# Twenty-one 8 KB buffers with 1 MB transfers, and 2 MB more of second-layer weights loaded early

## The chip, the cores and the metric

The kernel runs on one core of a Trainium2 chip. The metric is the device time of one execution in microseconds (us). Everything is fp32. The other cores of the chip have no part in it.

## The reference

Two things are computed one after the other. First a two-way attention between 512 tokens and 32 states, for 8 batches of 8 heads of width 64; then a soft mixture of experts over the 8 x (512 + 32) rows that come out, with 32 slots in 8 experts of 4.

```python
scores = scale * x @ state.T                # and the same scores the other way round
xread = softmax(scores, over states) @ state
sread = softmax(scores.T, over tokens) @ x
rows = concat([xread, sread])               # 4608 rows of 512
logits = rows @ phi                         # 512 x 32
slot_input = softmax(logits, over all rows).T @ rows
slot_out[e] = relu(slot_input[e] @ w1[e]) @ w2[e]     # w1: 8 x 512 x 1024, w2: 8 x 1024 x 512
out = softmax(logits, over slots) @ slot_out
```

The inputs are x (8.4 MB), the two weight tensors (16.8 MB each), the states and phi (0.6 MB); the output has 8.9 MB. Only x, the weights and the output matter for what follows.

## The kernel before

The program has four stages. The attention stage works through the 8 batches in an order that is written out by hand (the string `ORDER`, one step name per token); each engine executes its instructions in that order. A batch's step `R.b.1` is the last that reads the batch's x. The steps `Px`, `Ps` and `Y` towards the end of the stage gather the slot inputs, `windows` clears the two tiles `si_m` that hold them, and `SIe` fills these. The second stage multiplies them by the first-layer weights: `w1_part(hf, e)` for two halves `hf` of the hidden width and eight experts `e`, four matmul blocks each, 16 parts in all (matmuls at L650). The third stage multiplies by the second-layer weights: `w2_part(k, hf, e)` for four groups `k` of 128 output columns (matmuls at L710). The fourth, `out(k, q)` and `out_st(k)`, is interleaved with the third: it multiplies the combine weights by the slot outputs (L740), copies the result from PSUM by ScalarE (L749) and VectorE (L750), and stores it (L751).

All loads and nearly all stores are issued by SyncE (SP) in program order, and SP waits where a transfer's place or its source isn't ready. Two of the four transfers of the first batch's x are issued by ScalarE. The on-chip places for x, weights and outputs come from one pool, `big`: 43 buffers of 4 KB per partition (128 partitions, so 512 KB each), used in turn. One of them holds the states (`stT_sb`), 16 hold x (two per batch), and the remaining 26 take the first weights. Each weight tile is one transfer of 512 KB with rows of 4 KB per partition; 32 of them are w1, 32 are w2. After that a load waits for a place that comes free: `load_w(2)` follows each batch's `R.b.1`, one `load_w(1)` follows the last step that reads the states (`S.7` and `U.1`; the index `last` in the code), and `load_w(2)` follows each `w1_part`. So 43 weight tiles are on their way before the first `w1_part` frees a place: all 32 of w1, 11 of w2. The outputs take places of the same pool, two tiles and two stores of 512 KB for each `out(k, q)`.

Besides `big` there are the pool `wk` with 11 work tiles of 2 KB per partition under the tag `h` (the function `half`), and two tiles of 2 KB with the tags `srN` and `st`: turned read sums and turned states, last read by the steps `Ps.1` (L581) and `Px.3` (L501).

Of the kernel before, what the change touches and what calls it, by code (L numbers as in the profile page):

```python
# [8 lines left out]
F32 = mybir.dt.float32  # L9
# [6 lines left out]
P = 128  # L16
B = 8
S = 512
NS = 32
D = 64  # L20
E = 8
F = 1024
NJ = S // P
EPS = 1e-9
NBIG = 43
NH = 11


# [36 lines left out]
def attention_soft_moe(ctx: ExitStack, tc: tile.TileContext, x, stT, phi, w1, w2, out_x, out_s):  # L65
# [6 lines left out]
    nc = tc.nc  # L72
    pe, act, dve, pool = nc.tensor, nc.scalar, nc.vector, nc.gpsimd

    cp = ctx.enter_context(tc.tile_pool(name="const", bufs=1))
    ctx.enter_context(tc.manual_schedule())
    big = ctx.enter_context(tc.tile_pool(name="big", bufs=NBIG))


    stT_sb = big.tile([P, 4, 2, 2, 2, NS], F32, tag="big", name="stT_sb")  # L80
    phi_sb = cp.tile([P, 4, NS], F32, name="phi_sb")
    xb = []
    for b in range(B):
        for k in range(2):
            t = big.tile([P, 2, NJ, 2 * D], F32, tag="big", name=f"x{b}_{k}")
            xv = x[b].rearrange("p (g j c) -> p g j c", g=4, j=NJ)
            if b == 0:
                for g, eng in enumerate((nc.sync, act)):
                    eng.dma_start(t[:, g], xv[:, 2 * k + g])
            else:  # L90
                nc.sync.dma_start(t, xv[:, 2 * k : 2 * k + 2])
            xb.append(t)
        if b == 0:
            nc.sync.dma_start(stT_sb[:, 0:1], stT[:, 0:1])
        if b == 1:
            nc.sync.dma_start(stT_sb[:, 1:4], stT[:, 1:4])
            nc.sync.dma_start(phi_sb, phi)


    w1t, w2t = {}, {}  # L100
    todo = [(1, hf, e, k) for hf in range(2) for e in range(E) for k in range(2)]
    todo += [(2, k, e, 0) for k in range(4) for e in range(E)]

    def load_w2(t, k, e, ft):
        n = t.shape[1] // P
        t = t.rearrange("p (k f) -> p k f", k=n)
        nc.sync.dma_start(t, w2[e, k, :, ft : ft + n, :])
        for i in range(n):
            w2t[k, e, ft + i] = t[:, i]

    def load_w(n):
        for _ in range(min(n, len(todo))):
            layer, hf, e, k = todo.pop(0)
            t = big.tile([P, F], F32, tag="big", name=f"w{layer}_{hf}_{e}_{k}")
            if layer == 1:
                t = t.rearrange("p (k f) -> p k f", k=2)
                nc.sync.dma_start(t, w1[hf, e, :, 2 * k : 2 * k + 2, :])
                for i in range(2):
                    w1t[hf, e, 2 * k + i] = t[:, i]
            else:  # L120
                load_w2(t, hf, e, k)

    def st_t(b, g):
        return stT_sb[:, b // 2, g % 2, g // 2, b % 2, :]
# [2 lines left out]
    ident = cp.tile([P, P], F32, name="ident")  # L127
# [28 lines left out]
    with ExitStack() as actx:  # L156
        wk = actx.enter_context(tc.tile_pool(name="work", bufs=1))
# [14 lines left out]
        def half(name):  # L172
            return wk.tile([P, S], F32, tag="h", name=name, bufs=NH)

        def mtile(shape, name):
            return ps_m.tile(shape, F32, tag="ms", name=name)
# [24 lines left out]
        def X(b, g):  # L201
            r = R[b]
            r[f"xp{g}"] = p = ps_t.tile([P, S], F32, tag="tr", name=f"xt_ps{b}_{g}")
            for j in range(NJ):
                pe.transpose(p[:, P * j : P * j + P], xb[2 * b + g // 2][:, g % 2, j, :], ident)  # L205

        def xe(b, g):
            r = R[b]
# [100 lines left out]
        def R_(b, h):  # L309
            r = R[b]  # L310
            if h == 0:
                r["srp"] = mtile([P, 2, D], f"sr_ps{b}")
            for j in range(NJ):
                for g in range(4):
                    pe.matmul(  # L315
                        r["srp"][32 * g : 32 * g + 32, h, :],
                        r[f"eT{h}"][:, j, 32 * g : 32 * g + 32],
                        xb[2 * b + g // 2][:, g % 2, j, D * h : D * h + D],
                        start=(j == 0),
                        stop=(j == NJ - 1),  # L320
                    )
            if h == 1:
                load_w(2)

        def sr(b):
            r = R[b]
# [295 lines left out]
        def warm(n):  # L622
            p = ps_t.tile([P, S], F32, tag="tr", name=f"warm{n}_ps")
            pe.matmul(p[:, 0:n], ident, ident4[:, 0 : n // P], start=True, stop=True)

        steps = dict(
            G=G, Ge=Ge, X=X, xe=xe, S=Sc, q=q, m1=m1, sub=sub, x1=x1, l1=l1, r1=r1, mul=mul, aT=aT, m2=m2, e2=e2,
            l2=l2, E=E_, ee=ee, A=A_, ae=ae, R=R_, sr=sr, srT=srT, srTe=srTe, Lx=Lx, keep=keep, mx=mx, mk=mk,
            pv=pv, bm=bm, nme=nme, al=al, dx=dx, Lu=Lu, dT=dT, dTe=dTe, T=T_, tt=tt, U=U, Ue=Ue, Px=Px, Y=Y,
            Ls=Ls, Lse=Lse, Lr=Lr, msx=msx, als=als, dsx=dsx, Lus=Lus, lkp=lkp, D=Dn, V=V, Ve=Ve, Ps=Ps, Ys=Ys,  # L630
            Wd=Wd, We=We, Yf=Yf, SI=SI, SIe=SIe, windows=windows, mkd=mkd, ad=ad, W=warm,
        )
        load_w(NBIG - 2 * B - 1)
        order = ORDER.split()

        last = max(order.index(f"S.{B - 1}"), order.index("U.1"))
        for i, step in enumerate(order):
            name, *args = step.split(".")
            steps[name](*map(int, args))
            if i == last:  # L640
                load_w(1)


        h_ps = [ps_s.tile([P, 512], F32, tag="sc", name=f"h_ps{i}") for i in range(2)]
# [3 lines left out]
        def w1_part(hf, e):  # L648
            for kt in range(4):
                pe.matmul(  # L650
                    h_ps[hf][32 * kt : 32 * kt + 32, :],
                    si_m[kt // 2][:, 256 * (kt % 2) + 32 * e : 256 * (kt % 2) + 32 * e + 32],
                    w1t[hf, e, kt],
                    start=(e == 0),
                    stop=(e == E - 1),
                )
            load_w(2)

        def h_copy(hf):
            h_sb[hf] = half(f"h_sb{hf}")  # L660
# [19 lines left out]
        c = [half(f"c{i}") for i in range(3)]  # L680
        c = [v[:, 0 : t.shape[1]].rearrange("p (t n) -> p t n", n=NS) for v, t in zip(c, c_t)]
# [24 lines left out]
        def w2_part(k, hf, e):  # L706
            if hf == 0 and e == 0:
                so[k] = ps_s.tile([P, P], F32, tag="sc", name=f"so_ps{k}")
            for i in range(4):
                pe.matmul(  # L710
                    so[k][32 * i : 32 * i + 32, :],
                    h_m[hf][:, 256 * i + 32 * e : 256 * i + 32 * e + 32],
                    w2t[k, e, 4 * hf + i],
                    start=(hf == 0 and e == 0),
                    stop=(hf == 1 and e == E - 1),
                )
            if hf:
                load_w(1)

        def so_copy(k):  # L720
# [13 lines left out]
        def out(k, q):  # L734
            hf, col = k // 2, 128 * (k % 2)
            o = [(ps_t if j % 2 else ps_m).tile([P, 512], F32, tag="tr" if j % 2 else "ms", name=f"o{k}_{q}_{j}")
                 for j in range(NJ)]
            for j in range(NJ):
                rows = slice(32 * j, 32 * j + 32)
                pe.matmul(  # L740
                    o[j],
                    so_r[hf][rows, col : col + 128],
                    lt_all[rows, 4 * q : 4 * q + 4, :].rearrange("p b s -> p (b s)"),
                    start=True,
                    stop=True,
                )
            for jp in range(2):
                ot = big.tile([P, 2, 512], F32, tag="big", name=f"out{k}_{q}_{jp}")
                act.copy(ot[:, 0, :], o[2 * jp])  # L749
                dve.tensor_copy(ot[:, 1, :], o[2 * jp + 1])  # L750
                nc.sync.dma_start(out_x[k, q, jp].rearrange("p (i s) -> p i s", i=2), ot)  # L751

        ot = []

# [20 lines left out]
        for hf in range(2):  # L775
            for e in range(E):
                w1_part(hf, e)
                if hf == 0 and e == 5:
                    for i in range(3):
                        c_exp(i)  # L780
                if hf == 1 and e == 1:
                    h_turn(0)
                    h_relu(0)
                    for i in range(3):
                        c_div(i)
                if hf == 1 and e == 6:
                    for i in range(3):
                        c_back(i)
            h_copy(hf)

        for k in range(2):
            for e in range(E):
                w2_part(k, 0, e)
                if k == 0 and e == 3:
                    h_turn(1)
                    h_relu(1)
        for e in range(E):
            w2_part(0, 1, e)
        so_copy(0)

        for k in range(1, 4):
# [12 lines left out]
            more(2 * E)  # L814
            so_copy(k)
        out(2, 1)
        so_sum(3)
        out_st(2)
# [29 lines left out]
```

## Time and profile before

| | us |
|---|---|
| median of 3 runs | 135.07 (134.54 to 135.18) |
| profiled execution, whole time | 135.0 |
| profiled execution, span of the instructions | 133.2 |
| outside the span | 1.8 |

| engine | busy us | share of the span |
|---|---|---|
| TensorE matmuls (PE) | 118.0 | 89% |
| VectorE (DVE) | 86.8 | 65% |
| ScalarE (ACT) | 78.6 | 59% |
| GpSimd (POOL) | 44.7 | 34% |

The 16 DMA engines moved 51.76 MB, 389 GB/s over the span; TensorE's granted clock was at its full level throughout the work (mean 0.972 of it, since it falls after the last matmul). Matmuls are pipelined, so a busy PE need not be PE at its peak. The page cuts the span into 40 equal slices of 3.33 us; the views of the trace can be asked for any stretch, counted in us from the span's start.

### The profile page before, as it was taken

Reading aid. Unit: us, or ns where it says so; the run is one execution under the profiler, and the core shown is the slowest. Engines: PE = TensorE matmul, PEld = TensorE weight load, DVE = VectorE, ACT = ScalarE, POOL = GpSimd, SP = SyncE. Lnnn points to the kernel's source line nnn. Section 1 sums busy time; section 2 is a strip of 40 time slices with the busy share of each in tenths; the row PEclk is TensorE's granted clock in tenths of the full one; section 3 lists DMA queues with packets and bytes.
Section 4 is the critical chain, followed back from the end, with each engine's and each line's share of the span. In section 5 each row is a group of like instructions: output and inputs, shape, how many; then the busy total and the mean of one; then the engine's idle time right before and its main releaser. Section 6 shows DMA issues by size and latency. Waiting matters only on the chain.

```text
span 133.2 us, 5068 instructions
## 1 busy us (share of the span) xinstructions
PE 118.0 (89%) x2112; PEld 83.6 (63%) x2112; DVE 86.8 (65%) x218; ACT 78.6 (59%) x193; POOL 44.7 (34%) x64
## 2 busy tenths in 40 slices
PE   5898999999999999999899999999997999999200
PEld 2647686787886867567677779833893575754000
DVE  2019899999999999999997575059700733416300
ACT  3149999999999989988957414100100834427300
POOL 3006273563938056088884109406100000000000
PEclk9999999999999999999999999999999999999855
DMA  3999999999999999999999986999999999999992
GB/s 85 312 408 418 421 413 419 414 413 413 416 418 413 422 412 421 417 418 413 419 411 426 406 360 235 316 422 414 416 424 416 407 426 413 411 414 418 414 414 92
DMA packets 14854, 51.76 MB, mean 389 GB/s; under 512 B 1648, under 2 KB 1904, under 8 KB 14832
## 3 DMA queue, kind: packets, MB, share of 16 engines
q1 hardware_dynamic: 14544, 50.93, 95.2%
q10 hardware_dynamic: 288, 0.52, 1.1%
q8 instruction: 16, 0.26, 0.7%
q14 instruction: 6, 0.05, 0.1%
HBM read 42.53 MB, written 8.91 MB: 386 GB/s over the span
## 4 chain that ended last, share of the span: by engine, by line
PE 40%; DVE 37%; DMA 8%; issue 4%; ACT 2%; POOL 2%; DVEq 1%; ACTq 0%; POOLq 0%
PE so_ps L710 11%; PE h_ps L650 11%; PE o L740 7%; DVE l1s L248 6%; DVE q L232 6%; DVE nm L268 6%; DVE m L237 5%; DVE aT L262 5%; DMA phi_sb<-phi_in 5%; DMA x<-x_in 3%; DVE r L253 2%; POOL q L241 2%; PE os L758 2%; PE t_ps L467 1%; PE an_ps L287 1%
## 5 line engine op out<-in xcount | busy, mean ns | idle before, releaser
L750 DVE COPY out<-o 128x512 f32<-128x512 f32 x16 | 10.3, 686 | 18.7 <-PE o L740 18.7
L241 POOL TENSOR_TENSOR q<-q,m 128x512 f32<-128x512 f32 x16 | 16.7, 1050 | 16.0 <-DVE m L237 6.2
L210 ACT ACTIVATE xt<-xt_ps 128x512 f32<-128x512 f32 x32 | 18.9, 617 | 4.9 <-PE xt_ps L205 4.8
L257 POOL TENSOR_TENSOR q<-q,r 128x512 f32<-128x512 f32 x16 | 16.7, 1048 | 8.2 <-ACT eT L295 2.3
L205 PE MATMUL xt_ps<-ident,x 128*128 128x128 f32 x128 | 18.8, 285 | 0.4 <-DMA x<-x_in 0.4
L205 PEld LDWEIGHTS xt_ps<-ident,x 128*128 128x128 f32 x128 | 14.9, 146 | 3.5 <-DMA x<-x_in 1.2
L710 PEld LDWEIGHTS so_ps<-w,h_m 128*32 128x32 f32 x512 | 13.8, 110 | 4.3 <-issue 4.2
L710 PE MATMUL so_ps<-w,h_m 128*32 128x128 f32 x512 | 15.5, 274 | 0.9 <-issue 0.9
L232 DVE STREAM_TRANSPOSE q<-sc 128x512 f32<-128x512 f32 x16 | 11.1, 695 | 7.1 <-PE sc L219 7.1
L650 PE MATMUL h_ps<-w,si_m 128*32 128x512 f32 x128 | 14.4, 594 | 0.1
L749 ACT COPY out<-o 128x512 f32<-128x512 f32 x16 | 8.6, 588 | 7.2 <-PE o L740 7.2
L273 ACT ACTIVATE e<-sc,nm 128x512 f32<-128x512 f32 x16 | 11.2, 704 | 1.2 <-DVE q L232 0.4
L650 PEld LDWEIGHTS h_ps<-w,si_m 128*32 128x32 f32 x128 | 9.1, 110 | 4.0 <-issue 2.9
L315 PE MATMUL sr_ps<-x,eT 128*32 128x64 f32 x512 | 10.5, 221 | 0.3 <-ACT eT L295 0.3
L262 DVE STREAM_TRANSPOSE aT<-q 128x512 f32<-128x512 f32 x16 | 10.7, 687 | 0.0
L248 DVE TENSOR_REDUCE l1s<-q 128x16 f32<-128x512 f32 x16 | 10.5, 655 | 0.3 <-ACT q L244 0.3
L244 ACT ACTIVATE q<-q 128x512 f32<-128x512 f32 x16 | 10.5, 655 | 0.1
L268 DVE TENSOR_REDUCE nm<-sc 128x1 f32<-128x512 f32 x16 | 10.5, 660 | 0.0
L237 DVE TENSOR_REDUCE m<-q 128x16 f32<-128x512 f32 x16 | 10.5, 659 | 0.0
L287 PE MATMUL eT_ps<-ident,e 128*128 128x128 f32 x64 | 10.0, 279 | 0.5 <-ACT e L273 0.5
L315 PEld LDWEIGHTS sr_ps<-x,eT 128*32 128x32 f32 x512 | 8.6, 110 | 2.5 <-ACT lt_all L357 0.8
L287 PE MATMUL an_ps<-ident,aT 128*128 128x128 f32 x64 | 9.9, 280 | 0.2 <-DVE aT L262 0.2
(119 smaller groups left out, 187.2 us busy)
## 6 DMA issues: line engine op xcount, KB each, us to landing
w<-w_in SPq DMA_DIRECT2D x64, 512.0 KB, 10.0
out_x<-out SPq DMA_DIRECT2D x16, 512.0 KB, 7.6
x<-x_in SPq DMA_DIRECT2D x14, 512.0 KB, 10.1
x<-x_in ACTq DMA_DIRECT2D x2, 256.0 KB, 4.8
x<-x_in SPq DMA_DIRECT2D x2, 256.0 KB, 4.5
out_s<-out_s SPq DMA_DIRECT2D x2, 256.0 KB, 7.0
stT_sb<-stT_in SPq DMA_DIRECT2D x1, 384.0 KB, 7.5
stT_sb<-stT_in SPq DMA_DIRECT2D x1, 128.0 KB, 5.6
```

What stands on the lines that cost most here:

```text
L205: pe.transpose(p[:, P * j : P * j + P], xb[2 * b + g // 2][:, g % 2, j, :], ident)
L210: act.mul(r[f"xt{g}"], r[f"xp{g}"], 0.125)
L232: dve.transpose(r[f"q{h}"], r[f"sp{h}"])
L237: dve.tensor_reduce(out=r[f"m1{h}"], in_=r[f"qv{h}"], axis=AX.X, op=ALU.max)
L241: pool.tensor_tensor(v, v, R[b][f"m1{h}"].broadcast_to([P, 16, NS]), op=ALU.subtract)
L248: dve.tensor_reduce(out=l1s[:, i, :, 0:1], in_=R[b][f"qv{h}"], axis=AX.X, op=ALU.add)
L262: dve.transpose(r[f"aT{h}"], r[f"q{h}"])
L268: dve.tensor_reduce(out=r[f"nm2{h}"], in_=r[f"sp{h}"], axis=AX.X, op=ALU.max, negate=True)
L287: pe.transpose(p[:, j, :], r[f"{src}{h}"][:, P * j : P * j + P], ident)
L315: pe.matmul(r["srp"][32 * g : 32 * g + 32, h, :], r[f"eT{h}"][:, j, 32 * g : 32 * g + 32], xb[2 * b + g // 2][:, g % 2, j, D * h : D * h + D],
L650: pe.matmul(h_ps[hf][32 * kt : 32 * kt + 32, :], si_m[kt // 2][:, 256 * (kt % 2) + 32 * e : 256 * (kt % 2) + 32 * e + 32], w1t[hf, e, kt], ...
L710: pe.matmul(so[k][32 * i : 32 * i + 32, :], h_m[hf][:, 256 * i + 32 * e : 256 * i + 32 * e + 32], w2t[k, e, 4 * hf + i], start=(hf == 0 an ...
```

## The change

The pool `big` gets 21 buffers of 8 KB per partition (1 MB each) in place of 43 of 4 KB; the states get a pool of their own, `one`, with a single buffer of 4 KB. The room is the same: 21 x 8 + 4 = 43 x 4 = 172 KB. A batch's x is one buffer; batch 0 is still loaded in four transfers of 256 KB, batch 1 in two of 512 KB, and the others in one of 1 MB. A w1 tile is one half and expert with all its four blocks; a w2 tile holds two experts of one `k`. Their transfers are 1 MB with rows of 8 KB. Each place where two tiles were loaded now loads one.

Behind `last`, the next two pairs of w2 (k=1, experts 2 and 3, and experts 4 and 5) are taken out of the list and loaded piece by piece: expert 2 into the states' place (512 KB, where one tile was loaded before), experts 3 and 4 into four further work tiles after the step `windows` (4 x 256 KB), and expert 5 into the tiles of `srN` and `st` after the whole order (2 x 256 KB). In the order on SP these stand behind the load that follows `R.7.1` and ahead of those that follow the `w1_part`s. So 23 MB of weights are on their way before the first `w1_part` frees a place, where it was 21.5 MB.

An `out(k, q)` fills one buffer of 1 MB; for k = 0 and 1 it is one store of 1 MB, for k = 2 and 3 two of 512 KB as before, now rows of 4 KB in an output of 8 KB per partition. The host reorders w2 and the output accordingly. The instructions of the compute engines, their order and their shapes stay as they were.

```diff
@@ -22,7 +22,7 @@
 F = 1024
 NJ = S // P
 EPS = 1e-9
-NBIG = 43
+NBIG = 21
 NH = 11
 
 
@@ -77,19 +77,22 @@
     big = ctx.enter_context(tc.tile_pool(name="big", bufs=NBIG))
 
 
-    stT_sb = big.tile([P, 4, 2, 2, 2, NS], F32, tag="big", name="stT_sb")
+    one = ctx.enter_context(tc.tile_pool(name="one", bufs=1))
+    stT_sb = one.tile([P, 4, 2, 2, 2, NS], F32, tag="one", name="stT_sb")
     phi_sb = cp.tile([P, 4, NS], F32, name="phi_sb")
     xb = []
     for b in range(B):
-        for k in range(2):
-            t = big.tile([P, 2, NJ, 2 * D], F32, tag="big", name=f"x{b}_{k}")
-            xv = x[b].rearrange("p (g j c) -> p g j c", g=4, j=NJ)
-            if b == 0:
-                for g, eng in enumerate((nc.sync, act)):
-                    eng.dma_start(t[:, g], xv[:, 2 * k + g])
-            else:
-                nc.sync.dma_start(t, xv[:, 2 * k : 2 * k + 2])
-            xb.append(t)
+        t = big.tile([P, 4, NJ, 2 * D], F32, tag="big", name=f"x{b}")
+        xv = x[b].rearrange("p (g j c) -> p g j c", g=4, j=NJ)
+        if b == 0:
+            for g in range(4):
+                (act if g % 2 else nc.sync).dma_start(t[:, g], xv[:, g])
+        elif b == 1:
+            for g in (0, 2):
+                nc.sync.dma_start(t[:, g : g + 2], xv[:, g : g + 2])
+        else:
+            nc.sync.dma_start(t, xv)
+        xb.append(t)
         if b == 0:
             nc.sync.dma_start(stT_sb[:, 0:1], stT[:, 0:1])
         if b == 1:
@@ -98,27 +101,30 @@
 
 
     w1t, w2t = {}, {}
-    todo = [(1, hf, e, k) for hf in range(2) for e in range(E) for k in range(2)]
-    todo += [(2, k, e, 0) for k in range(4) for e in range(E)]
-
-    def load_w2(t, k, e, ft):
+    todo = [(1, hf, e) for hf in range(2) for e in range(E)]
+    todo += [(2, k, e) for k in range(4) for e in range(0, E, 2)]
+
+    def load_w(n):
+        for _ in range(min(n, len(todo))):
+            layer, k, e = todo.pop(0)
+            t = big.tile([P, 2 * F], F32, tag="big", name=f"w{layer}_{k}_{e}")
+            if layer == 1:
+                t = t.rearrange("p (k f) -> p k f", k=4)
+                nc.sync.dma_start(t, w1[k, e])
+                for i in range(4):
+                    w1t[k, e, i] = t[:, i]
+            else:
+                t = t.rearrange("p (e k f) -> p e k f", e=2, k=8)
+                nc.sync.dma_start(t, w2[e // 2, k])
+                for i in range(16):
+                    w2t[k, e + i // 8, i % 8] = t[:, i // 8, i % 8]
+
+    def load_part(t, k, e, ft):
         n = t.shape[1] // P
         t = t.rearrange("p (k f) -> p k f", k=n)
-        nc.sync.dma_start(t, w2[e, k, :, ft : ft + n, :])
+        nc.sync.dma_start(t, w2[e // 2, k][:, e % 2, ft : ft + n])
         for i in range(n):
             w2t[k, e, ft + i] = t[:, i]
-
-    def load_w(n):
-        for _ in range(min(n, len(todo))):
-            layer, hf, e, k = todo.pop(0)
-            t = big.tile([P, F], F32, tag="big", name=f"w{layer}_{hf}_{e}_{k}")
-            if layer == 1:
-                t = t.rearrange("p (k f) -> p k f", k=2)
-                nc.sync.dma_start(t, w1[hf, e, :, 2 * k : 2 * k + 2, :])
-                for i in range(2):
-                    w1t[hf, e, 2 * k + i] = t[:, i]
-            else:
-                load_w2(t, hf, e, k)
 
     def st_t(b, g):
         return stT_sb[:, b // 2, g % 2, g // 2, b % 2, :]
@@ -315,12 +321,12 @@
                     pe.matmul(
                         r["srp"][32 * g : 32 * g + 32, h, :],
                         r[f"eT{h}"][:, j, 32 * g : 32 * g + 32],
-                        xb[2 * b + g // 2][:, g % 2, j, D * h : D * h + D],
+                        xb[b][:, g, j, D * h : D * h + D],
                         start=(j == 0),
                         stop=(j == NJ - 1),
                     )
             if h == 1:
-                load_w(2)
+                load_w(1)
 
         def sr(b):
             r = R[b]
@@ -630,15 +636,24 @@
             Ls=Ls, Lse=Lse, Lr=Lr, msx=msx, als=als, dsx=dsx, Lus=Lus, lkp=lkp, D=Dn, V=V, Ve=Ve, Ps=Ps, Ys=Ys,
             Wd=Wd, We=We, Yf=Yf, SI=SI, SIe=SIe, windows=windows, mkd=mkd, ad=ad, W=warm,
         )
-        load_w(NBIG - 2 * B - 1)
+        load_w(NBIG - B)
         order = ORDER.split()
 
+        pairs = []
         last = max(order.index(f"S.{B - 1}"), order.index("U.1"))
         for i, step in enumerate(order):
             name, *args = step.split(".")
             steps[name](*map(int, args))
             if i == last:
-                load_w(1)
+                pairs = [todo.pop(0)[1:] for _ in range(2)]
+                (k, e), (k2, e2) = pairs
+                load_part(one.tile([P, F], F32, tag="one", name=f"w2_{k}_{e}"), k, e, 0)
+            if name == "windows":
+                for k, e in ((k, e + 1), (k2, e2)):
+                    for ft in (0, 4):
+                        load_part(half(f"w2_{k}_{e}_{ft}"), k, e, ft)
+        for ft, tag in ((0, "srN"), (4, "st")):
+            load_part(wk.tile([P, S], F32, tag=tag, name=f"w2_{k2}_{e2 + 1}_{ft}", bufs=1), k2, e2 + 1, ft)
 
 
         h_ps = [ps_s.tile([P, 512], F32, tag="sc", name=f"h_ps{i}") for i in range(2)]
@@ -654,7 +669,7 @@
                     start=(e == 0),
                     stop=(e == E - 1),
                 )
-            load_w(2)
+            load_w(1)
 
         def h_copy(hf):
             h_sb[hf] = half(f"h_sb{hf}")
@@ -714,7 +729,7 @@
                     start=(hf == 0 and e == 0),
                     stop=(hf == 1 and e == E - 1),
                 )
-            if hf:
+            if hf and e % 2:
                 load_w(1)
 
         def so_copy(k):
@@ -744,11 +759,15 @@
                     start=True,
                     stop=True,
                 )
+            ot = big.tile([P, NJ, 512], F32, tag="big", name=f"out{k}_{q}")
             for jp in range(2):
-                ot = big.tile([P, 2, 512], F32, tag="big", name=f"out{k}_{q}_{jp}")
-                act.copy(ot[:, 0, :], o[2 * jp])
-                dve.tensor_copy(ot[:, 1, :], o[2 * jp + 1])
-                nc.sync.dma_start(out_x[k, q, jp].rearrange("p (i s) -> p i s", i=2), ot)
+                act.copy(ot[:, 2 * jp, :], o[2 * jp])
+                dve.tensor_copy(ot[:, 2 * jp + 1, :], o[2 * jp + 1])
+                if k > 1:
+                    two = slice(2 * jp, 2 * jp + 2)
+                    nc.sync.dma_start(out_x[k, q, :, two], ot[:, two])
+            if k < 2:
+                nc.sync.dma_start(out_x[k, q], ot)
 
         ot = []
...
```

## Rows read from the trace of the kernel before

**Rows 1.** The page: TensorE's busy time, and the DMA's busy share and rate by slice

```profile
PE 118.0 (89%) x2112; PEld 83.6 (63%) x2112; DVE 86.8 (65%) x218; ACT 78.6 (59%) x193; POOL 44.7 (34%) x64
DMA  3999999999999999999999986999999999999992
GB/s 85 312 408 418 421 413 419 414 413 413 416 418 413 422 412 421 417 418 413 419 411 426 406 360 235 316 422 414 416 424 416 407 426 413 411 414 418 414 414 92
```

**Rows 2.** Stretches: length, busy us by engine (count), clock, DMA share, GB/s

```profile
20.00:40.00 20.00, 19.76 (x410) 15.59 (x409) 19.71 (x50) 19.87 (x48) 10.49 (x11) 1.00 1.03 416
78.00:80.00 2.00, 1.87 (x18) 1.65 (x21) 1.97 (x7) 0.00 (x0) 0.04 (x1) 1.00 0.77 311
80.00:82.00 2.00, 2.00 (x25) 1.89 (x20) 1.89 (x4) 0.63 (x1) 1.77 (x2) 1.00 0.79 281
82.00:84.00 2.00, 2.00 (x24) 1.87 (x20) 0.00 (x0) 0.99 (x2) 2.00 (x4) 1.00 0.73 199
84.00:86.00 2.00, 2.00 (x25) 1.87 (x20) 0.00 (x0) 0.38 (x1) 0.64 (x1) 1.00 0.84 320
86.00:88.00 2.00, 2.00 (x21) 0.97 (x16) 0.07 (x1) 0.21 (x1) 0.00 (x0) 1.00 1.01 408
88.00:126.00 38.00, 34.36 (x644) 21.04 (x636) 17.81 (x38) 12.31 (x29) 2.71 (x3) 1.00 1.03 417
129.00:130.00 1.00, 0.00 (x0) 0.00 (x0) 0.00 (x0) 0.00 (x0) 0.00 (x0) 0.50 0.93 379
130.00:131.00 1.00, 0.00 (x0) 0.00 (x0) 0.00 (x0) 0.00 (x0) 0.00 (x0) 0.50 0.51 209
131.00:132.00 1.00, 0.00 (x0) 0.00 (x0) 0.00 (x0) 0.00 (x0) 0.00 (x0) 0.50 0.16 66
```

**Rows 3.** SP's waits, whole span: total us, times, longest

```profile
SPq L107 <- DMA w<-w_in: 23.7, 24, 2.4
SPq L751 <- DVE out L750: 15.8, 14, 3.7
SPq L107 <- PE h_ps L650: 9.0, 9, 5.9
```

**Rows 4.** First load after the wait; landing times of L107, then of L117

```profile
79.41 0.33 SPq L107 DMA_DIRECT2D w<-w_in  x1
DMA to landing us min/median/max: 4.1/10.8/11.5
DMA to landing us min/median/max: 9.8/10.0/10.0
```

**Rows 5.** The end: TensorE, copies, stores, and the last two stores' landing

```profile
118.12 1.14 PE L740 MATMUL o<-lt_all,so_r 32*128 32x512 f32 x8
120.08 3.38 SPq L751 DMA_DIRECT2D out_x<-out  x4
123.58 1.29 DVE L750 COPY out<-o 128x512 f32<-128x512 f32 x2 [0.51 <-PE o L740]
L751 SPq DMA_DIRECT2D out_x<-out x2: 630/831/1032, 124.4 to 125.5; - x2
DMA to landing us min/median/max: 6.7/6.8/6.8
```

**Rows 6.** When the new places come free; first-layer matmuls in the chain

```profile
70.14 0.98 POOL L616 MEMSET si_m<- 128x512 f32 x2
75.51 0.59 PE L581 MATMUL ps_ps<-srN,D 128*32 128x128 f32 x8
76.34 0.44 PE L501 MATMUL px_ps<-st,tt 64*32 64x64 f32 x16
78.24 9.06 PE h_ps L650 x80
```

**Rows 7.** Batch 2 of x: first reader, and landing of the loads from 5.2

```profile
15.68 0.63 PE L205 MATMUL xt_ps<-ident,x 128*128 128x128 f32 x4
DMA to landing us min/median/max: 6.8/6.9/7.7
```

**Rows 8.** The page's code loads (packets, MB, share); TensorE's wait that nothing explains

```profile
q8 instruction: 16, 0.26, 0.7%
PE so_ps L710 <- issue: 0.9, 1, 0.9
```

More of the change, by code (lines that the diff above doesn't have):

```diff
@@ L204, in X @@
             for j in range(NJ):
-                pe.transpose(p[:, P * j : P * j + P], xb[2 * b + g // 2][:, g % 2, j, :], ident)
+                pe.transpose(p[:, P * j : P * j + P], xb[b][:, g, j, :], ident)
         def xe(b, g):
@@ L835 @@
         "w1_in": con(moe_w1.reshape(E, 4, P, 2, 512).transpose(3, 0, 2, 1, 4)),
-        "w2_in": con(moe_w2.reshape(E, 8, P, 4, P).transpose(0, 3, 2, 1, 4)),
+        "w2_in": con(moe_w2.reshape(E // 2, 2, 8, P, 4, P).transpose(0, 4, 3, 1, 2, 5)),
     }
@@ L839 @@
     args = [nc.dram_tensor(n, a.shape, F32, kind="ExternalInput").ap() for n, a in arrays.items()]
-    args.append(nc.dram_tensor("out_x", (4, 2, 2, P, 2 * 512), F32, kind="ExternalOutput").ap())
+    args.append(nc.dram_tensor("out_x", (4, 2, P, 4, 512), F32, kind="ExternalOutput").ap())
     args.append(nc.dram_tensor("out_s", (2, P, 512), F32, kind="ExternalOutput").ap())
@@ L844 @@
     r = _run(nc, [arrays], core_ids=[0]).results[0]
-    ox = r["out_x"].reshape(4, 2, 2, P, 2, 4, P).transpose(1, 5, 2, 4, 6, 0, 3).reshape(B, S, 512)
+    ox = r["out_x"].reshape(4, 2, P, 2, 2, 4, P).transpose(1, 5, 3, 4, 6, 0, 2).reshape(B, S, 512)
     os_ = r["out_s"].reshape(2, P, 2, B, NS).transpose(3, 4, 0, 2, 1).reshape(B, NS, 512)
```

## The prediction

> **What bounds the kernel now.** Read first the slices of the page [rows 1]: from the third slice to the last but one the DMA's busy share stands at its ceiling, except in four slices around 80 us. The kernel moves 51.76 MB, and at the 416 GB/s of an undisturbed stretch [rows 2] that alone is 124 us of a span of 133.2. TensorE is busy for 118.0 us too [rows 1], so both are close to the end, and the question is which of them a change lets go first.
>
> Then the stretches [rows 2]. From 20 to 40 the rate is 416 GB/s and from 88 to 126 it is 417; in the five stretches from 78 to 88 it is 311, 281, 199, 320 and 408. Missing against 416: 105, 135, 217, 96 and 8 GB/s, each for 2 us, which divided by 416 is 0.50 + 0.65 + 1.04 + 0.46 + 0.04 = **2.7 us** of DMA work not done. Why it is missing stands in SP's waits [rows 3]: nine times a load of L107 waited for the first-layer matmuls, 5.9 us of it in one piece. That piece ends with the load issued at 79.41 [rows 4]: 43 weight tiles were on their way, every place was taken, and the first came free when the first `w1_part` was done, one part after 78.24 (80 matmuls, ten parts, in 9.06 us, so 0.9 us each [rows 6]). SP's other waits in the load stage (23.7 us in 24 pieces, at most 2.4 [rows 3]) are for landings of earlier loads: a landing takes 10.0 us [rows 4] at 1.26 us for 512 KB (512 KB by 416 GB/s), so eight transfers are under way at a time. These waits cost nothing, since the DMA is full meanwhile.
>
> Last the end [rows 5]. TensorE starts the matmuls of `out(2, 1)` at 118.12; their stores are issued from 120.08. The last copies run from 123.58, the last store is issued at 125.5, and lands 6.8 us later, at 132.3. With nothing queued, the shortest landing of 512 KB is 4.1 us [rows 4]. So the last store stood in a queue: the end is set by the DMA, by up to 2.7 us, and behind it TensorE with its copies sets the next limit. The rest of the span, 133.2 - 132.3 = 0.9 us, and 1.8 us outside it stay. The DMA engines don't end together either: in the three last stretches their share is 0.93, 0.51 and 0.16 [rows 2].
>
> **The change part by part.** *Two more megabytes.* Before, 21.5 MB of weights were on their way before the first place came free; now it is 23 MB (of the 2 MB, the 0.5 in the states' place were there already). The added 1.5 MB are 1.57 million bytes, 3.8 us of DMA work at 416 GB/s, against 2.7 us that are missing. Are they issued in time? The four work tiles can be taken once `windows` is reached in the order (its clearing starts at 70.14), the tile `srN` after 75.51 + 0.59 = 76.1, the tile `st` after 76.34 + 0.44 = 76.8 [rows 6]. The queue ran dry only past 78 [rows 2]. Behind these six pieces on SP stand only the loads for the places of the `w1_part`s, the first of which can't go before 79.1 anyway; nobody else waits on SP. With eight under way, the first load for a freed place waits for the landing of the eighth before it, the 1 MB load that follows `R.7.1`; then 2 MB (4.8 to 5 us) are still queued, enough. So the gap closes: -2.7 us for the DMA. The weights loaded early are wanted by the second layer only, many microseconds later.
>
> *1 MB transfers with 8 KB rows.* Half as many transfers, the same bytes in the same order. No row shows an 8 KB row on SP's queue. The nearest is the 4 KB row at 416 GB/s; As bounds I take a gain and a loss of 3.6%, 4.5 us of the 124, which is how far full slices of one row size lie apart (411 and 426 [rows 1]). The value I take is 0, that of the nearest row, since the DMA's share is full with 4 KB already. A gain would not be seen whole: see the limit by the outputs below. A loss would be: it is counted with slower. The Trainium skill (DMA: Bandwidth & Descriptors, Rules for kernel authors) asks for 1 MiB per DMA for the best bandwidth, and in its section on one DMA's anatomy gives about 2.0 us fixed for each; by that estimate some 37 fewer transfers would save 74 us. Here the trace disagrees: transfers of 512 KB follow each other every 1.26 us, with the fixed part hidden by the eight under way, so there is none of it to save.
>
> *x in one piece.* Batches 2 to 7 land as a whole; the first half is 1.26 us later than before. Batch 2's two loads are the first two from 5.2 and land 6.8 to 6.9 us after issue, the first at about 12.1, the second 1.26 us behind it at about 13.4; its first reader starts at 15.68 [rows 7]. Slack 2.3 us, growing for later batches, as a batch's x comes every 2.5 us and the stage, which ends at 78.24 [rows 6], takes (78.24 - 15.68) / 8 = 7.8 us for one. Cost 0; without that cover it would be 1.26 us once.
>
> *Work tiles, pools, outputs.* Four of 11 work tiles hold weights until the third stage. Behind `windows` the tiles taken are 2 + 4 + 3 (`c`) + 2 (`h_sb`) = 11, so nobody waits for one before it is read. Stores of 1 MB for k = 0 and 1 go out one VectorE copy, 1.29 / 2 = 0.65 us [rows 5], later than their first half did, while the queue is still full of weights. Cost 0, or 0.65 us if the queue is empty there. Compute instructions don't change.
>
> **The sum, with two limits.** By the DMA: 132.3 - 2.7 = 129.6. By the outputs: from 120.08 on there remain six stores of 512 KB and one of 256 KB, 3.4 MB, 8.2 us. They can't begin before the issue at 120.08 plus what a store needs ahead of its data: at most 4.1 - 1.26 = 2.8 us, at least 0. The 4.1 us were measured while some engines still worked on older loads (share 0.77 and 0.79 from 78 to 82 [rows 2]), so I take the middle, 1.5: 120.08 + 1.5 + 8.2 = 129.8 (128.3 to 131.1). A last store alone gives 125.5 + 4.1 = 129.6. All meet near 129.7. The later limit, 129.8, plus 0.9 and 1.8 gives **132.5 us**, against 135.0 of the profiled execution, which stands at the median of 135.07. So what closes the gap is gained nearly whole, and then the DMA and the outputs share the bound.
>
> **Rivals.** *Deeper gain* (12 in 100): 8 KB rows raise the rate, and TensorE's one wait of 0.9 us at L710 [rows 8] goes, so that the outputs come earlier by it: 132.5 - 0.9 = 131.6. Against it: nothing in the change takes that wait away.
>
> *A shallow queue at the end or a gap only half closed* (17 in 100). From 82 to 84 the rate was 199 GB/s although loads had been going out since 79.41: a queue that has run empty is slow to fill. If the weights are through early and the queue runs dry before 120.08, that happens again, 1.0 us [rows 2]: 133.5; a gap half closed gives 132.5 + 1.35 = 133.9.
>
> *It doesn't do what it says* (7 in 100). In the gap some DMA engines went on with older loads. If the engine that ends last is one that never stood, little is gained there: between 135.0 and the 134.4 that is still no change.
>
> *Slower by code loads* (4 in 100, and 2 for long rows that lose 3.6%: the DMA's limit is then 129.6 + 4.5 = 134.1, the time 136.8). The page has 16 code loads that took 0.7% of 16 x 133.2 us, 0.93 us each for 16 KB [rows 8]; at 416 / 16 = 26 GB/s of one engine 16 KB are 0.63 us, so about 0.3 us go to data packets between. With rows twice as long that may double: 0.3 us more for each. TensorE did stand once for 0.9 us for nothing that the profile names. If it stands for all 16, that is 4.8 us: 132.5 + 4.8 = 137.3; slower than before from nine of them on (2.7 us). Against it: the rest of TensorE's idle time is small, 34.36 of 38 us busy from 88 to 126 [rows 2], and most of that has other causes. The Trainium skill (DMA: Bandwidth & Descriptors, Queues, rings and completion order) says that an engine drains a whole packet of one queue before it turns to the next; the 0.93 us against 0.63 agree with that, and no run shows it for 8 KB.
>
> **How the numbers follow.** The forecast, 131.9 to 133.2, has 58 in 100. The range 131.2 to 134.2 takes in the deeper gain and the shallow queue and leaves out no change and slower. What a measurement of this kernel can tell from no change is about 0.5%, so faster means under 134.4 and slower over 135.7: faster 58 + 12 + 17 less one for the edge = 86, same 8, slower 6.
>
> **What would show it.** In the profile after: the four slices around 80 us at 410 GB/s or more; SP's wait of L107 for the first-layer matmuls gone or under 1 us; first reader of batch 2 still near 15.7; `out(2, 1)` stored from about 120; the landing of the last stores near 4 to 5 us where it was 6.8; in slices 35 to 38 a dip where the outputs, not the DMA, set the pace. Wrong would be: the dip filled and the last landing still at 132 (the engine that ends last had no gap), matmuls of the third stage starting later than 78.24 + 16 x 0.9 = 92.7 or standing more than 0.9 us with no releaser (code loads), or a steady rate below 405 GB/s (long rows are slower).

## The result, and the profile after

| | before | changed |
|---|---|---|
| median, us | 135.06 (134.54 to 135.18) | 133.05 (133.04 to 133.13) |
| span of the profiled execution, us | 133.2 | 131.3 |
| TensorE matmuls busy, us | 118.0 | 118.1 |
| data moved over the span, GB/s | 389 | 394 |

The ratio is 0.9859 with a 95% interval of 0.9834 to 0.9885: 1.4% faster by the ratio, 2.0 us by the medians. Forecast was 132.5 us, with a range of 131.2 to 134.2.

The slices of the page, as in [rows 1] (DMA busy share in tenths, and GB/s):

```profile
DMA  3899999999999999999999999999999899797992
GB/s 77 316 386 439 422 422 427 419 432 414 424 422 422 429 414 427 434 422 427 419 422 422 417 415 398 428 414 429 427 424 417 372 397 414 320 399 307 419 414 120
```

The hole around 80 us (360, 235 and 316 GB/s in the 24th to 26th slice before) is filled: 415, 398, 428. In its place there are shallow ones from 104 us on, where none was before: 372, 320 and 307 in the 32nd, 35th and 37th slice. The steady rate is higher too. By stretches, the columns as in [rows 2]:

```profile
20.00:40.00 20.00, 19.73 (x409) 15.65 (x409) 19.71 (x50) 19.82 (x48) 10.56 (x11) 1.00 1.01 423
80.00:82.00 2.00, 2.00 (x24) 1.86 (x20) 1.72 (x4) 0.63 (x1) 1.71 (x2) 1.00 1.08 402
82.00:84.00 2.00, 2.00 (x24) 1.89 (x20) 0.00 (x0) 0.99 (x2) 2.00 (x4) 1.00 1.02 407
104.00:108.00 4.00, 4.00 (x52) 1.97 (x51) 2.48 (x5) 2.76 (x8) 0.00 (x0) 1.00 0.88 363
112.00:116.00 4.00, 3.76 (x76) 2.45 (x80) 2.55 (x4) 2.62 (x6) 0.00 (x0) 1.00 0.78 326
116.00:120.00 4.00, 3.76 (x87) 2.62 (x76) 0.87 (x2) 1.18 (x3) 0.00 (x0) 1.00 0.97 385
120.00:124.00 4.00, 3.57 (x20) 1.30 (x19) 2.33 (x5) 2.71 (x8) 0.00 (x0) 1.00 0.87 354
120.00:120.50 0.50, 0.50 (x6) 0.13 (x7) 0.42 (x1) 0.37 (x3) 0.00 (x0) 1.00 0.12 49
120.60:120.70 0.10, 0.10 (x4) 0.10 (x4) 0.00 (x0) 0.10 (x1) 0.00 (x0) 1.00 0.10 41
120.70:120.80 0.10, 0.10 (x4) 0.00 (x0) 0.00 (x0) 0.10 (x1) 0.00 (x0) 1.00 1.08 451
128.00:129.00 1.00, 0.00 (x0) 0.00 (x0) 0.00 (x0) 0.00 (x0) 0.00 (x0) 0.50 0.88 361
129.00:130.00 1.00, 0.00 (x0) 0.00 (x0) 0.00 (x0) 0.00 (x0) 0.00 (x0) 0.50 0.05 20
```

From 104 to 124 TensorE is busy for nearly all of the time, and the DMA is not: against 416 GB/s, the four stretches lack 53, 90, 31 and 62 GB/s for 4 us each, 0.5 + 0.9 + 0.3 + 0.6 = 2.3 us. From 120.0 to 120.5, behind the issue of `out(2, 1)`'s first store at 119.89, the share is down to 0.12: the queue has run dry and waits for outputs, until it is full again at 120.7. The idle time has moved from one side of the second layer to the other. The wait that was removed, in SP's waits (total us, times, longest):

```profile
SPq L118 <- PE h_ps L665: 1.2, 4, 0.5
SPq L770 <- DVE out L765: 24.0, 4, 16.8
```

The load line (L118, before L107) waits for the first-layer matmuls 1.2 us in all, where it was 9.0 and 5.9 in one piece [rows 3]. Instead SP waits for VectorE's copies of outputs, 16.8 us in one piece: its loads are issued long before the outputs are there. The end, as in [rows 5]: TensorE's matmuls of `out(2, 1)`, their stores, the landing of the first of these, and the last two stores with their landing:

```profile
117.93 1.14 PE L755 MATMUL o<-lt_all,so_r 32*128 32x512 f32 x8
119.89 3.38 SPq L768 DMA_DIRECT2D out_x<-out  x4
DMA to landing us min/median/max: 3.6/3.6/3.6
L768 SPq DMA_DIRECT2D out_x<-out x2: 537/810/1084, 124.1 to 125.3; - x2
DMA to landing us min/median/max: 4.9/4.9/4.9
```

The matmuls stand 0.2 us earlier than before (118.12), the stores as well (120.08). The last landing took 6.8 us and takes 4.9: the queue that the last store stood in is gone, and the copies set the pace.

### The profile page after: what moved, and what is told of

It reads as the page before. It is cut to its first block, busy times and chain, and to the rows that moved or that the text cites. A ratio compares the mean times of both kernels' runs of the same rounds, so it can differ in the third digit from the quotient of the medians.

```text
span 131.3 us, 4990 instructions
## 1 busy us (share of the span) xinstructions
PE 118.1 (90%) x2112; PEld 84.0 (64%) x2112; DVE 86.7 (66%) x218; ACT 78.6 (60%) x193; POOL 44.8 (34%) x64
## 4 chain that ended last, share of the span: by engine, by line
PE 45%; DVE 38%; ACT 4%; issue 4%; DMA 3%; DVEq 0%; ACTq 0%
PE so_ps L725 11%; PE h_ps L665 11%; PE o L755 7%; DVE q L238 6%; DVE l1s L254 6%; DVE nm L274 6%; DVE m L243 5%; DVE aT L268 5%; DMA x<-x_in 3%; PE xt_ps L211 3%; DVE r L259 3%; PE t_ps L473 2%; PE os L777 2%; PE an_ps L293 1%; PE sc L225 1%
## 5 line engine op out<-in xcount | busy, mean ns | idle before, releaser
L247 POOL TENSOR_TENSOR q<-q,m 128x512 f32<-128x512 f32 x16 | 16.8, 1051 | 16.0 <-DVE m L243 6.1
```

The costliest lines, as they stand in the source:

```text
L247: pool.tensor_tensor(v, v, R[b][f"m1{h}"].broadcast_to([P, 16, NS]), op=ALU.subtract)
```

## The experiments

Each of the experiments was timed against the kernel before on the same chip; its median lay between 134.26 and 134.66 in these comparisons, so the ratios count more than the microseconds. The kernel before spreads by 1.6 to 1.9 us within each of them, the changed kernel by 0.6 us in its eight runs further down. **First theory** (the prediction's): closing the gap gives the gain, long rows give none, and behind the gap the outputs limit it. **Rival**: the changed kernel moves 423 GB/s where it was 416; the long rows give the gain, or would give it as well.

**Long rows alone.** The pieces into work tiles and turned sums are left out; the other half of the one pair goes into the first freed buffer, by a branch in `load_w` that is left out here:

```diff
...
-                pairs = [todo.pop(0)[1:] for _ in range(2)]
-                (k, e), (k2, e2) = pairs
+                _, k, e = todo.pop(0)
                 load_part(one.tile([P, F], F32, tag="one", ...), k, e, 0)
-            if name == "windows":
...
+                todo.insert(0, (0, k, e + 1))
```

> The changed kernel without its 1.5 MB of additional early weights: 21 buffers, transfers of 1 MB with rows of 8 KB, 21.5 MB on their way before the first freed place as in the kernel before; one half pair of w2 goes into the states' place, its other half into the first freed buffer. Theory of the prediction (the gap is what is gained, long rows are worth 0): the gap around 80 us is back and so is the time, 134.7 to 135.1. Second theory (the rate of 423 to 425 GB/s that the changed kernel shows from 20 to 60 is worth 2% of some 100 us of weight loads, about 2 us, and the outputs hold the end from there): the gap is back, the weights are still through early enough, 133.0 to 133.6.

Measured: 134.98 us, ratio 1.0047 (1.0007 to 1.0086). Nothing is gained. The stretches around the gap, and SP's longest wait:

```profile
20.00:40.00 20.00, 19.71 (x408) 15.53 (x408) 19.71 (x50) 19.73 (x48) 10.44 (x11) 1.00 1.01 422
78.00:80.00 2.00, 1.87 (x19) 1.64 (x21) 1.96 (x7) 0.00 (x0) 0.03 (x1) 1.00 0.42 168
80.00:82.00 2.00, 2.00 (x24) 1.89 (x19) 1.91 (x4) 0.63 (x1) 1.77 (x2) 1.00 0.72 178
82.00:84.00 2.00, 2.00 (x24) 1.86 (x20) 0.00 (x0) 0.99 (x2) 2.00 (x4) 1.00 0.95 285
SPq L127 <- PE h_ps L661: 11.0, 1, 11.0
```

And from 76 to 90, which holds the whole gap, the kernel before and this run:

```profile
76.00:90.00 14.00, 13.85 (x131) 10.17 (x133) 6.79 (x23) 2.61 (x5) 4.45 (x5) 1.00 0.89 338
76.00:90.00 14.00, 13.80 (x132) 10.17 (x132) 6.90 (x22) 2.61 (x5) 4.45 (x5) 1.00 0.86 324
```

The rate is 422 GB/s, as in the changed kernel. But against 422 this run lacks 98 / 422 x 14 = 3.3 us from 76 to 90, where the kernel before lacks 78 / 416 x 14 = 2.6 against its 416. Faster loads fill the same places earlier and then wait longer for the first freed one, which comes when TensorE has done a part, not when the DMA is ready. So of the 0.9 us by which 422 against 416 GB/s is ahead after 60 us of loads, some 0.6 is lost in the gap. How much of this is the rate's doing is not shown: in this run the first freed place takes only 512 KB, where two loads of 512 KB followed before. The rest of the lead brought nothing either; in this profile TensorE stood for 1.3 us with no releaser where it stood for 0.9 before [rows 8], and the last store was issued 0.6 us later. The rival's 133.0 to 133.6 is out.

**Early weights alone.** The kernel before, with three more w2 tiles loaded into the six pieces:

```diff
             if i == last:
                 load_w(1)
+                early = [todo.pop(0)[1:3] for _ in range(3)]
+            if name == "windows":
+                for k, e in early[:2]:
+                    for ft in (0, 4):
+                        load_w2(half(f"w2_{k}_{e}_{ft}"), k, e, ft)
+        k, e = early[2]
+        for ft, tag in ((0, "srN"), (4, "st")):
+            load_w2(wk.tile([P, S], F32, tag=tag, ...), k, e, ft)
```

> The kernel before (43 buffers, transfers of 512 KB, rows of 4 KB) with the 1.5 MB of w2 loaded early into four work tiles and the two tiles of turned sums and states. Theory of the prediction: the gap closes, the rate stays at 416 to 417 GB/s, and the DMA's limit of 129.6 and the outputs' limit meet: 132.4 to 133.2. Theory that the long rows carry the gain: at most a part is gained, 134.0 to 135.0.

Measured: 133.01 us, ratio 0.9885 (0.9819 to 0.9951): the gain of the change as far as these runs can tell (its ratio was 0.9859, and 0.9909 in the repetition below), with the old buffers, transfers and rate. SP's wait and the stretches:

```profile
SPq L107 <- PE h_ps L659: 1.1, 4, 0.3
20.00:40.00 20.00, 19.70 (x408) 15.51 (x407) 19.71 (x50) 19.74 (x48) 10.53 (x11) 1.00 1.03 416
82.00:84.00 2.00, 2.00 (x24) 1.89 (x20) 0.00 (x0) 0.99 (x2) 2.00 (x4) 1.00 1.06 398
104.00:108.00 4.00, 4.00 (x60) 1.98 (x56) 2.48 (x5) 2.76 (x7) 0.00 (x0) 1.00 1.03 415
120.00:124.00 4.00, 3.35 (x19) 1.28 (x18) 2.33 (x5) 2.71 (x7) 0.00 (x0) 1.00 0.98 400
```

The gap is closed at 398 GB/s from 82 to 84, and the DMA is full up to 116 us and nearly so after it: the DMA's limit and the outputs' limit meet here, as the sum had it for a rate of 416.

**What raises the rate.** The changed kernel with the same 1 MB weight transfers, each partition's 8 KB taken from two separate rows of 4 KB in memory (the host's layout and the loads of pieces follow, not shown):

```diff
-                nc.sync.dma_start(t, w1[k, e])
+                nc.sync.dma_start(t.rearrange("p (r k) f -> p r (k f)", r=2), w1[k, e].rearrange("r p f -> p r f"))
...
-                nc.sync.dma_start(t, w2[e // 2, k])
+                nc.sync.dma_start(t.rearrange("p e k f -> p e (k f)"), w2[e // 2, k].rearrange("e p f -> p e f"))
```

> The changed kernel with the weights' transfers still of 1 MB, but cut into two rows of 4 KB per partition by the host's layout. If the length of the rows sets the rate, 416 to 417 GB/s from 30 to 60 us; if the number of transfers does, 423 to 425. The time by the outputs' limit hardly moves in either case: 132.9 to 133.4.

Measured: 133.16 us, ratio 0.9899 (0.9833 to 0.9966). The stretch from 40 to 60, when only weights are loaded:

```profile
40.00:60.00 20.00, 19.26 (x396) 13.74 (x394) 19.68 (x52) 18.27 (x49) 9.94 (x11) 1.00 1.03 418
```

418 GB/s, against 425 in the changed kernel and 417 before in the same stretch. So most of the rate, 7 of 8 GB/s, comes with the length of the row; halving the number of transfers gave 1. And the time is the changed kernel's as far as these runs can tell: 133.16 us against 133.05 and, in the repetition below, 133.23. Since only the rows differ here, this is the cleanest measure that long rows are worth nothing in the changed kernel.

**Does TensorE's way to the outputs hold the end?** In both kernels 7 of the 16 second-layer parts of k = 2 and of k = 3 are left out:

```diff
         def w2_part(k, hf, e):
+            if k > 1 and e % 2 and (hf, e) != (1, 7):
+                return
```

> The changed kernel without 7 of the 16 second-layer parts of each of the output groups k = 2 and 3 (odd experts; their matmuls are left out, their weights are loaded all the same). TensorE's way to the outputs is shorter by 7 x 0.23 = 1.6 us before out(2, 1) and its successors for each of the two groups, 3.2 us in all. If the outputs hold the end: the time falls until the DMA's limit is reached (weights through at about 106, then 8.9 MB at 416 GB/s, 21.4 us, so 127.5 to 128.5): 131.0 to 131.8. If the DMA holds the end: unchanged at 133.0.

> The kernel before without the same 7 of 16 second-layer parts for k = 2 and 3. The DMA held the end there by the prediction: unchanged, 134.8 to 135.2. If TensorE's way to the outputs held it there too, the time falls by 1 us or more.

Measured: the changed kernel 132.01 us, ratio to the full kernel before 0.9798 (0.9736 to 0.9859); the kernel before 134.37, ratio 0.9962 (0.9927 to 0.9998). With 3.2 us less on TensorE the other kernel gives 0.3 us, and the changed one about 1.0; the changed kernel itself was timed on other chips, so that by the ratios (0.9859 and 0.9909 for the changed kernel in full) it is 0.8 to 1.5. So TensorE does limit the changed kernel and hardly the old one, but by less than I had put: the changed kernel was expected at 131.0 to 131.8. From 104 to 108 its DMA stands as before, since the first outputs come no earlier; behind that it is full:

```profile
104.00:108.00 4.00, 4.00 (x48) 1.97 (x50) 2.48 (x5) 2.76 (x8) 0.00 (x0) 1.00 0.86 354
112.00:116.00 4.00, 4.00 (x88) 2.32 (x84) 1.29 (x2) 1.58 (x4) 0.00 (x0) 1.00 0.99 414
120.00:124.00 4.00, 0.83 (x6) 0.00 (x0) 1.29 (x2) 1.07 (x2) 0.00 (x0) 0.70 1.02 411
```

**Copies by pairs.** The copies and stores of an output's first half are written behind its first two matmul blocks:

```diff
-            for j in range(NJ):
-                rows = ...
-                pe.matmul(o[j], ...)
             for jp in range(2):
+                for j in (2 * jp, 2 * jp + 1):
+                    rows = ...
+                    pe.matmul(o[j], ...)
                 act.copy(ot[:, 2 * jp, :], o[2 * jp])
```

> The changed kernel with the copies and stores of an output's first half written right behind the first two of its four matmul blocks. If the outputs hold the end, as I hold, the stores from out(2, 1) on are issued up to 0.55 us earlier (half of 1.1 us of matmuls) and the time falls by 0.2 to 0.5 us, to 132.5 to 132.9. If the DMA holds the end, nothing changes: 133.0 to 133.1.

Measured: 133.17 us, ratio 0.9927 (0.9886 to 0.9967), no gain. The edit didn't bring what it was for, as TensorE's and ScalarE's lines of `out(2, 1)` show:

```profile
118.28 1.14 PE L757 MATMUL o<-lt_all,so_r 32*128 32x512 f32 x8
119.44 1.07 ACT L764 COPY out<-o 128x512 f32<-128x512 f32 x2 [0.70 <-PE o L757]
```

The first copy still starts 1.16 us behind the first matmul, when all eight instructions are through; it is 119.09 - 117.93 = 1.16 in the changed kernel. So this run says nothing on the limit. The stretches of that line alone (length, TensorE's matmuls and weight loads, clock, DMA share, GB/s) show what may lie behind it:

```profile
118.28:118.40 0.12, 0.12 (x4) 0.12 (x6) 1.00 0.91 375
119.00:119.10 0.10, 0.10 (x4) 0.00 (x0) 1.00 1.19 410
```

The eight records of 0.6 us each run four at a time: the first four start together at 118.28, the other four are under way until the end at 119.4. That the four blocks run side by side, so that none is ready much before the others, fits the late copy; which record is which block the trace doesn't say.

**Outputs moved inside.** `out(1, 1)` and `out(2, 1)` go into the middle of the next group's second-layer parts:

```diff
         for k in range(1, 4):
-            if k == 1:
-                more(3)
+            if k == 2:
+                out(0, 1)
             else:
-                out(k - 2, 1)
+                more(3)
             so_sum(k - 1)
...
             out(k - 1, 0)
+            if k > 1:
+                more(8)
+                out(k - 1, 1)
             more(2 * E)
             so_copy(k)
-        out(2, 1)
-        so_sum(3)
         out_st(2)
+        so_sum(3)
```

> The changed kernel with out(1, 1) and out(2, 1) moved into the middle of the next group's second-layer parts, so that stores are issued while the DMA would stand. If the outputs hold the end by the DMA's idle time between 104 and 124 us and by the engine that was late through a code load at 118, the idle stretches are filled and the end is set by out(3, 0), issued about 122.5: 132.0 to 132.8. If the last stores' own path holds it, 133.0 to 133.3.

Measured: 132.17 us, ratio 0.9822 (0.9754 to 0.9891). It was run again beside the changed kernel on one chip:

> The changed kernel itself, beside the version with two outputs moved inside, on the same chip. 133.0 to 133.2, a ratio of 0.985 to 0.990 to the kernel before.

> The version with out(1, 1) and out(2, 1) inside the next group's second-layer parts, beside the changed kernel on the same chip. If it is really better than the changed kernel: 0.8 to 1.0 us below it. If the 0.9 us lay between the chips: within 0.3 us of it.

Measured: 133.23 us, ratio 0.9909 (0.9874 to 0.9944), and 132.20 us, ratio 0.9837 (0.9797 to 0.9878). The changed kernel gains less here than in its first comparison, and its ratio just misses the expected 0.985 to 0.990: 1.0 us by the medians where it was 2.0, since the kernel before ran at 134.26 on this chip and at 135.06 on the first. So the gain of the change is known as 1 to 2 us, less than the 2.5 of the forecast. On the same chip the move gives 1.0 us more, with the same work on every engine. The stretches of the second profile, and from 104 to 124 those of the changed kernel and of this one:

```profile
112.00:116.00 4.00, 4.00 (x93) 2.79 (x85) 0.88 (x2) 1.82 (x5) 0.00 (x0) 1.00 1.02 422
116.00:120.00 4.00, 4.00 (x87) 2.52 (x80) 1.70 (x3) 1.59 (x5) 0.00 (x0) 1.00 0.90 359
120.00:124.00 4.00, 3.42 (x20) 1.38 (x19) 1.65 (x3) 2.30 (x6) 0.00 (x0) 1.00 0.75 305
104.00:124.00 20.00, 19.10 (x326) 11.38 (x321) 8.81 (x15) 9.92 (x25) 0.00 (x0) 1.00 0.90 369
104.00:124.00 20.00, 19.42 (x334) 11.63 (x326) 9.00 (x15) 10.29 (x25) 0.00 (x0) 1.00 0.90 368
```

From 112 to 116 the DMA is full (326 GB/s in the changed kernel); it stands later instead, from 116 to 124, ahead of `out(3, 0)`. Over the whole 20 us it stands as long as before, 369 and 368 GB/s, so other than expected the move did not fill the idle stretches. What is shorter is the end, by the stretches and the last two stores' landing:

```profile
128.00:129.00 1.00, 0.00 (x0) 0.00 (x0) 0.00 (x0) 0.00 (x0) 0.00 (x0) 0.50 1.01 418
129.00:129.25 0.25, 0.00 (x0) 0.00 (x0) 0.00 (x0) 0.00 (x0) 0.00 (x0) 0.50 0.27 99
129.25:129.50 0.25, 0.00 (x0) 0.00 (x0) 0.00 (x0) 0.00 (x0) 0.00 (x0) 0.50 0.00 0
DMA to landing us min/median/max: 3.9/4.0/4.1
```

All engines end together at 129.1, and the last store lands 4.1 us after its issue, where it was 4.9. In the changed kernel most engines end at 128.9, but one goes on to 129.8 (see the two limits below).

**Both.** Copies by pairs in that version:

> The changed kernel with both the outputs moved inside and the copies by pairs. If the two effects add: 131.6 to 132.5. If the last stores' path alone holds the end, the time of the better of the two.

Measured: 132.29 us, ratio 0.9811 (0.9760 to 0.9861): the time of the better of the two.

**Are long rows worth something then?** The same move in the kernel with early weights alone:

> The kernel with early weights alone (43 buffers, 512 KB transfers, 4 KB rows) and the two outputs moved inside, as in the version that came to 132.2. If long rows are worth something once the outputs come early enough, the DMA's limit at 416 GB/s (129.6 for the last landing, 132.3 in all) holds it: 132.5 to 133.0, no gain or little over the same kernel without the move (133.0). If long rows are worth nothing there either: 132.0 to 132.3.

Measured: 132.86 us, ratio 0.9894 (0.9855 to 0.9933). In the kernel with rows of 4 KB the move gives 0.15 us (133.01 to 132.86, on two chips) or nothing by the ratios (0.9885 and 0.9894), in the changed kernel 1.0. So the two kernels with the move differ by 0.7 us, at ratios of 0.9894 and 0.9837 whose intervals just touch. That this is the worth of long rows is not shown: the two also differ in the number of transfers and in x, and no run has the move with 1 MB in rows of 4 KB.

## Why the prediction was right, step by step

*The bound.* The DMA's gap from 78 to 88 was the thing to gain, read from the stretches and from SP's one long wait; the run with early weights alone shows it with nothing else changed. The 1.5 MB covered it (the title's 2 MB count the 0.5 MB that went into the states' place before as well).

*Long rows.* Their value in the sum was 0, and the kernel with long rows alone bears it out. The step that led there was not quite right: I took the rate itself as unchanged, with bounds of 3.6% to both sides, and it rose by 423 / 416, 1.7%. That the time didn't follow has two reasons: where the gap is left open, the run with long rows alone had a longer gap, which the prediction didn't have; where it is closed, the outputs aren't ready, which it had. The rule of the Trainium skill on 1 MiB per transfer (DMA: Bandwidth & Descriptors, Rules for kernel authors) is not borne out for a queue that holds some eight transfers (the prediction's estimate from the landings): 1 MB in 4 KB rows ran at 418 GB/s, 512 KB at 417. The 2.0 us for each transfer that the prediction takes from the same page are its figure for transfers issued by GpSimd; these are issued by SyncE, and a store behind a dry queue took 0.8 + 0.45 = 1.25 us beside its data (see the two limits).

*x in one piece, work tiles.* Nothing shows. The first reader of batch 2 starts at 15.80, before at 15.68 [rows 7]; TensorE's busy time is the same.

*The two limits.* The mechanism is as predicted: the queue runs dry and the outputs set the end. The size was off by 0.55 us. Stores from 119.89 on (predicted 120.08), the last landing at 125.33 + 4.9 = 130.25 (predicted 129.8): +0.45. From the last landing to the end of the span 131.3 - 130.25 = 1.05 (0.9): +0.15. Outside the span 133.05 - 131.3 = 1.75 (1.8): -0.05. The mis-sized term is the landing of the remaining 3.4 MB. The DMA is at its full rate again from 120.7 on, 0.8 us behind the issue, and most engines are done 8.2 us later, at 128.9, as the sum had it. The share from 129 to 130 is 0.05: of 16 engines that is one, busy for 0.8 us when all others are done. Its last packet goes at 129.8, and 0.45 us later the store counts as landed. So the 1.5 us that a store needs beside its data came out as 0.8 + 0.45, near the middle of a wide range (0 to 2.8), which is luck; the late engine's 0.9 us were missing, since the sum counted the engines as one. A code load fell into the time before; the DMA views (queue, packets, MB, share of 16 engines) of the stretches from 117.9 to 118.5, from 119.9 to 120.7 and from 129 to 130:

```profile
q1 hardware_dynamic: 60, 0.24, 98.3%
q8 instruction: 1, 0.02, 9.9%
q1 hardware_dynamic: 13, 0.04, 11.6%
q1 hardware_dynamic: 7, 0.02, 5.1%
```

Its 0.099 x 16 x 0.6 us = 0.95 us lie on one engine. In the second stretch, where the queue is dry, 13 packets still go: 0.116 x 16 x 0.8 = 1.5 us of work for one or two engines that are behind, until just before the new stores start at 120.7. So an engine could carry its lag over this short pause to the end. In the version with outputs moved inside the DMA stands at a share of 0.31 for the 1.5 us from 122 to 123.5, and there no engine is late at the end. All this fits the code load as the cause, but it is argued from the sizes; the trace doesn't name engines, and no run moved a code load alone.

*Rivals.* The deeper gain came by neither of its parts: the rate rose, and TensorE's wait at the second layer stayed (0.8 us, before 0.9 [rows 8]). A half closed gap: no, the gap's stretches are at 401 to 439 GB/s. The shallow queue at the end: its condition came true, since the queue ran dry at 119.8, ahead of 120.08, but the refill wasn't slow; the DMA was full 0.8 us behind the issue of the first store. That the engine that ends last had no gap: no, the time fell. Code loads slowed by long rows: their share is the page's 0.7% for 16 in both kernels (0.9 us each), so no loss from rows twice as long can be seen, and the Trainium skill's rule on whole packets (DMA: Bandwidth & Descriptors, Queues, rings and completion order) costs nothing here within that rounding.

*The marks.* Third-stage matmuls were to start by 92.7 or else something was wrong; they start at 92.8 (93.0 before), and nothing is wrong: the mark left out the four turns of the hidden values (0.59 us) that stand between. The landing of 4 to 5 us, the first reader and the stores from about 120 came as written, the others nearly so: one of the four slices around 80 us has 398 GB/s, not 410; SP's wait for the first-layer matmuls is 1.2 us in four pieces, not under 1; and the dips lie in slices 32, 35 and 37, the first of them outside the 35 to 38 of the mark.

## What to carry to other kernels

When the DMA is full except in one hole, look for what ends the hole: here it was a place to put data, so more places closed it, and a faster DMA alone gained nothing. Work out the next limit in the same way before counting the gain: by the sum two limits here lay within 0.2 us of each other, so neither a higher rate nor shorter compute was worth its size alone. Read the end engine by engine: moving two outputs gave 1.0 us with the DMA idle for as long as before, and what differed in the profile was that no engine was late at the end.

## What the runs showed of the hardware

Rows of 8 KB per partition moved at 422 to 426 GB/s in transfers of 1 MB, and rows of 4 KB at 416 to 418 in transfers of 512 KB or of 1 MB alike (stretches from 20 to 60 us, one core at work). The 16 DMA engines end apart: before, the share fell from 0.93 to 0.16 over the last three microseconds with data [rows 2]; after the change one engine ran 0.9 us longer than the rest. An end counted from the mean rate is early by that much. Behind a dry queue the DMA was at full rate 0.8 us after the issue of a store, and a store counted as landed 0.45 us after its last packet (changed kernel, 119.89 to 120.7 and 129.8 to 130.25).
